# Gated attention feeding two expert layers on one core: scores issued behind the previous chunk's outputs, transposes of keys on their own, and PSUM shared out anew

## The chip, the cores and the metric

The kernel runs on one core of a Trainium2 chip. The metric is the device time of one execution in microseconds (us); before the change it is 919.28 us, the median of 3 runs (918.77 to 920.1). TensorE is called PE, VectorE DVE, ScalarE ACT, GpSimd POOL and SyncE SP.

## The reference

```python
f = 1 / (1 + exp(-f_logit))
for t in range(S):                                   # attention: B=4, H=8, S=768, D=48
    state = f[:, :, t, :, None] * state + k[:, :, t] (x) v[:, :, t]
    y[:, :, t] = q[:, :, t] @ state
x = y.transpose(0, 2, 1, 3).reshape(B * S, H * D)    # 3072 tokens, 384 wide
x = maximum(x @ w_in, 0)**2 @ w_out                  # layer 1, 384 -> 2048 -> 384
h = x @ w_in2                                        # layer 2, the same sizes
return where(h > 0, h, exp(minimum(h, 0)) - 1) @ w_out2
```

## The kernel before, in words

**Attention** is computed in 24 chunks g of 128 tokens, each with all 8 heads of one batch (batch g % 4), so the state that chunk g needs is that of chunk g-4. Heads lie in four pairs p, the two heads of a pair on partitions 0 to 47 and 64 to 111. For a chunk, `a_gate` and `a_decay` turn the logits into running products of decays, `a_scale` (L168) multiplies queries and keys by them, and `a_scores` first transposes the keys (L176, tile tp, four transposes) and then multiplies keys by queries (L182, tile sc, one matmul for each head). `a_transposed` (L187) copies tp to SBUF on ACT (kt), `a_mask` (L191) copies the causal half of the scores into ss on DVE. `a_carry` (L196) decays the state, `a_state` (L209) multiplies keys by values (tile kv), `a_add` (L218) adds that to the state on DVE. `a_out` sums two products into tile o: masked scores by values (L241) and state by queries (L248); ACT copies o to SBUF (L255), small DMAs on SP's queue put it in its place (L260), and `a_hi` and `a_lo` (L280, L288) split it into the two parts xh and xl that the layers read. Every fp32 matmul is issued as two instructions.

**The layers** run in 12 blocks of 512 tokens (6 of each layer) by 16 pieces f of 128 hidden features, 192 units in all. The main loop (L485 to L498) has one slot u for each unit: first the planned steps of slot u, then `up` of unit u (L360, nine matmuls of 128x128 by 512 columns into tile ph), `down` of unit u-2 (L412, nine matmuls into the three banks y), then `between` of unit u (L373 to L379 in layer 1: relu and square on ACT, gh on ACT in block 0) and `low` (gl; on DVE, L393, in block 0, on POOL, L399, later). In block 0 the weights of unit u+1 are also unpacked: `load_raw` (DMA), `decode_weights` (L52 on ACT, then L54, L57 and L58 on DVE, tile dec) and `split_weights`, whose high part is a copy on ACT (L329) and whose low part is a subtraction on DVE (L330) that reads the high part.

**The order** within an engine is the order of issue, written by hand: a table START for the first chunks and units, then `plan`, a list of steps for each slot. The table FIRST says at which slots of a block a chunk's steps begin (at 0, 3, 6 and 8 for chunks 4 to 7, all in block 0; for the chunks whose tokens block i takes, at -6, -2, 2 and 6 counted from the start of block i-1); the steps then follow slot by slot: gate, decay, scale and carry, (an empty slot,) scores with transposes and mask, state and outputs, add, nothing, hi and lo. Within a slot, the steps of chunks are issued ahead of those of the weights.

**PSUM**'s eight banks: two for ph of layer 1 (`ps_h`), three for y0, y1 and y2 (`ps_y`), and three in turn (`ps_a`) for everything else: tp, the two halves of sc, kv, the two halves of o, and ph of layer 2.

Of the kernel before, what the change touches and what calls it, by code (L numbers as in the profile page):

```python
# [11 lines left out]
F32 = mybir.dt.float32  # L12
# [24 lines left out]
FIRST = (0, 3, 6, 8), (-6, -2, 2, 6)  # L37
# [23 lines left out]
def chunked(ctx, tc, ff, qk, vk, vz, wraw, mask, ident, flag, out):  # L61
# [15 lines left out]
    ps_h = ctx.enter_context(tc.tile_pool(name="ps_h", bufs=2, space=PSUM))  # L77
    ps_y = ctx.enter_context(tc.tile_pool(name="ps_y", bufs=1, space=PSUM))
    ps_a = ctx.enter_context(tc.tile_pool(name="ps_a", bufs=3, space=PSUM))
# [89 lines left out]

    def a_scores(g):  # L170
        s = st[g]
        q, k = (s["qk"][:, o].rearrange("r (p t) -> r p t", p=NP) for o in range(2))
        if g < NG - B:
            s["tp"] = tp = ps_a.tile([128, NP, 128], F32, tag="a", name=f"tp{g}")
            for p in range(NP):
                PE.transpose(tp[:, p, 0:ROWS], k[:, p], idt[:ROWS, :ROWS])  # L176

        pool, tags = (ps_a, "aa") if g >= B else (ps_h, "hh") if g % 2 else (ps_y, ("y0", "y1"))
        s["sc"] = sc = [pool.tile([128, NP, 128], F32, tag=tags[j], name=f"sc{g}_{j}") for j in range(2)]
        for p in range(NP):  # L180
# [17 lines left out]
    def a_state(g):  # L198
        s = st[g]
        now = state[g % B]  # L200
        if g < NG - B:
            kvp = ps_a.tile([128, NP, 48], F32, tag="a", name=f"kv{g}")
            for p in range(NP):
                for j, (lo, hi) in enumerate(((0, 64), (64, ROWS))):
                    if g >= B:
                        v = s["vk"][:, p, j]
                    else:
                        v = s["vz"][:, p, at_(p, j), 0:48] if p < NK else s["vz"][:, :, at_(p, j), 96:112]
                    PE.matmul(kvp[lo:hi, p], s["kt"][:, p, lo:hi], v, start=True, stop=True)  # L209
            if g >= B:  # L210
                s["kv"] = kvp
            else:
                A.activation(now, kvp[:ROWS], AF.Copy)

    def a_add(g):
        if g < NG - B:
            now = state[g % B]
            V.tensor_tensor(out=now, in0=st[g]["kv"][:ROWS], in1=now, op=ALU.add)  # L218

    def a_direct(g):  # L220
        s = st[g]
        yp = ps_a.tile([128, NK, 128], F32, tag="a", name=f"yp{g}")
# [9 lines left out]
    def a_out(g):  # L232
# [20 lines left out]
        for i in (1, 0):  # L253
            for lo, hi in HD:
                A.activation(x1[lo:hi, 2 * i:2 * i + 2], o[i][lo:hi], AF.Copy)  # L255
# [405 lines left out]
```

## Time and profile before

| | before |
|---|---|
| runs | 920.1, 918.77, 919.28 us; median 919.28 |
| the profiled execution's own time | 917.91 us |
| its span | 916.1 us |
| PE busy | 890.3 us (97%) |
| DVE busy | 562.4 us (61%) |
| ACT busy | 440.8 us (48%) |
| POOL busy | 295.2 us (32%) |
| mean granted TensorE clock | 0.990 |

The profile is of one execution. Its span runs from the first to the last instruction; 1.8 us of the execution's own time lie around it. An engine's busy time counts the instructions that work on data; matmuls are pipelined, so the rows of PE overlap by the end of each. In a row of the timeline that stands for several instructions (x16), the first number is the start of the first, the second the time from there to the end of the last. Idle time stands at the end of a row in brackets, with what ended it.

### The profile page before, as it was taken

Reading aid. Unit: us, or ns where it says so; the run is one execution under the profiler, and the core shown is the slowest. Engines: PE = TensorE matmul, PEld = TensorE weight load, DVE = VectorE, ACT = ScalarE, POOL = GpSimd, SP = SyncE. Lnnn points to the kernel's source line nnn. Section 1 sums busy time; section 2 is a strip of 40 time slices with the busy share of each in tenths; the row PEclk is TensorE's granted clock in tenths of the full one; section 3 lists DMA queues with packets and bytes.
Section 4 is the critical chain, followed back from the end, with each engine's and each line's share of the span. In section 5 each row is a group of like instructions: output and inputs, shape, how many; then the busy total and the mean of one; then the engine's idle time right before and its main releaser. Section 6 shows DMA issues by size and latency. Waiting matters only on the chain.

```text
span 916.1 us, 13300 instructions
## 1 busy us (share of the span) xinstructions
PE 890.3 (97%) x5001; PEld 724.5 (79%) x5001; DVE 562.4 (61%) x837; ACT 440.8 (48%) x751; POOL 295.2 (32%) x243
## 2 busy tenths in 40 slices
PE   7799899999999999999999999999999999999997
PEld 5577688888888888788888888888888888888885
DVE  8899978677676676775300256555564565555543
ACT  4477655444544444444444444444544444444543
POOL 2111114444444344442333233332333323333231
PEclk8999999999999999999999999999999999999999
DMA  8556434334344533433256510100100100100001
GB/s 265 165 177 200 140 105 145 110 112 145 112 129 148 180 128 110 146 112 109 110 184 224 189 59 0 58 12 1 58 11 1 58 12 1 57 12 1 35 1 38
DMA packets 30791, 88.45 MB, mean 97 GB/s; under 512 B 4992, under 2 KB 9728, under 8 KB 30720
## 3 DMA queue, kind: packets, MB, share of 16 engines
q1 hardware_dynamic: 28848, 77.32, 25.5%
q10 hardware_dynamic: 1872, 10.22, 3.3%
q8 instruction: 40, 0.66, 0.3%
q14 instruction: 31, 0.25, 0.1%
HBM read 64.52 MB, written 22.02 MB: 94 GB/s over the span
## 4 chain that ended last, share of the span: by engine, by line
PE 92%; DVE 4%; DMA 1%; issue 1%; ACT 1%; SPq 0%; DVEq 0%
PE ph L360 42%; PE y L412 42%; PE sc L182 3%; PE o L241 2%; PE o L248 1%; DMA ff<-ff 1%; PE kv L209 1%; PE tp L176 1%; DVE ds L145 1%; DVE dec L57 1%; DVE w L330 0%; DVE qk L168 0%; PE yp L226 0%; DVE dec L58 0%; DVE gl L393 0%
## 5 line engine op out<-in xcount | busy, mean ns | idle before, releaser
L399 POOL TENSOR_TENSOR gl<-gg,gh 128x512 fp32r<-128x512 f32 x175 | 250.0, 1429 | 500.1 <-PE ph L360 192.2
L412 PE MATMUL y<-gh,wf 128*128 128x512 f32 (+1 forms) x582 | 177.9, 387 | 0.0
L412 PE MATMUL y<-gh,w 128*128 128x512 f32 x576 | 177.4, 389 | 0.0
L385 DVE SCALAR_TENSOR_TENSOR t<-r,t 128x512 f32<-128x512 f32 (+1 forms) x97 | 71.9, 742 | 158.8 <-ACT r L384 158.5
L360 PE MATMUL ph<-xh,w 128*128 128x512 f32 x576 | 155.5, 405 | 4.9 <-DVE w L330 3.1
L360 PE MATMUL ph<-xh,wf 128*128 128x512 f32 (+1 forms) x582 | 146.4, 387 | 0.0
L381 ACT ACTIVATE r<-ph 128x512 f32<-128x512 f32 (+1 forms) x97 | 57.6, 593 | 181.9 <-PE ph L360 177.0
L360 PEld LDWEIGHTS ph<-xh,w 128*128 128x128 f32 x576 | 106.0, 190 | 34.0 <-DVE w L330 4.6
L412 PEld LDWEIGHTS y<-gh,wf 128*128 128x128 f32 x582 | 108.9, 188 | 22.4 <-ACT gh L388 0.2
L360 PEld LDWEIGHTS ph<-xh,wf 128*128 128x128 f32 x582 | 108.6, 188 | 22.3
L412 PEld LDWEIGHTS y<-gh,w 128*128 128x128 f32 x576 | 108.1, 188 | 22.5
L412 PE MATMUL y<-gl,wf 128*128 128x512 f32 (+1 forms) x291 | 112.7, 387 | 0.0
L373 ACT ACTIVATE r<-ph 128x512 f32<-128x512 f32 x96 | 57.1, 595 | 114.6 <-PE ph L360 94.7
L412 PE MATMUL y<-gl,w 128*128 128x512 f32 x288 | 112.1, 389 | 0.0
L360 PE MATMUL ph<-xl,w 128*128 128x512 f32 x288 | 81.7, 392 | 1.9 <-DVE xl L286 1.9
L360 PE MATMUL ph<-xl,wf 128*128 128x512 f32 (+1 forms) x291 | 81.1, 387 | 0.0
L379 DVE TENSOR_TENSOR gh<-r 128x512 fp32r<-128x512 f32 x64 | 45.8, 716 | 49.4 <-ACT r L373 49.3
L386 DVE SCALAR_TENSOR_TENSOR gg<-ph,t 128x512 f32<-128x512 f32 (+1 forms) x97 | 66.6, 686 | 10.0
L360 PEld LDWEIGHTS ph<-xl,w 128*128 128x128 f32 x288 | 54.6, 190 | 14.2 <-DVE xl L286 2.4
L374 ACT ACTIVATE gg<-r 128x512 f32<-128x512 f32 x96 | 60.7, 633 | 7.7
L412 PEld LDWEIGHTS y<-gl,wf 128*128 128x128 f32 x291 | 54.6, 188 | 11.2 <-DVE gl L393 0.2
L360 PEld LDWEIGHTS ph<-xl,wf 128*128 128x128 f32 x291 | 54.4, 188 | 11.1
(73 smaller groups left out, 959.4 us busy)
## 6 DMA issues: line engine op xcount, KB each, us to landing
raw<-wraw SPq DMA_DIRECT2D x19, 768.0 KB, 4.7
wst<-w SPq DMA_DIRECT2D x16, 768.0 KB, 4.3
wf<-wst SPq DMA_DIRECT2D x16, 768.0 KB, 4.2
qk<-qk SPq DMA_DIRECT2D x24, 448.0 KB, 5.7
raw<-wraw ACTq DMA_DIRECT2D x13, 768.0 KB, 4.5
ff<-ff SPq DMA_DIRECT2D x22, 227.9 KB, 4.8
x2d<-yo SPq DMA_DIRECT2D x18, 256.0 KB, 2.3
x<-x2d SPq DMA_DIRECT2D x18, 256.0 KB, 3.2
```

The source lines that it names most:

```text
L57: V.scalar_tensor_tensor(out=out, in0=hi, scalar=0x80000000, in1=out, op0=ALU.bitwise_and, op1=ALU.bitwise_or)
L182: PE.matmul(sc[j][:, p], k[lo:hi, p], q[lo:hi, p], start=True, stop=True)
L241: PE.matmul(o[p // 2][r:r + 48, p % 2], s["vk"][:, p, j], ss[g % 2][:, j, p], start=p % 2 == 0, stop=False, skip_group_check=True,)
L360: PE.matmul(ph, w[:, a, 0, 128 * k:128 * k + 128], b[:, k, c], start=(m == 0), stop=(m == len(todo) - 1))
L373: A.activation(r[:, c], ph, AF.Relu)
L374: A.activation(gg[:, c], r[:, c], AF.Square)
L379: V.tensor_tensor(out=gh[:, c], in0=r[:, c], in1=r[:, c], op=ALU.mult)
L381: A.activation(r[:, c], ph, AF.Relu, scale=-1.0)
L385: V.scalar_tensor_tensor(out=t[:, c], in0=r[:, c], scalar=1.0, in1=t[:, c], op0=ALU.add, op1=ALU.mult)
L386: V.scalar_tensor_tensor(out=gg[:, c], in0=ph, scalar=0.0, in1=t[:, c], op0=ALU.max, op1=ALU.add)
L399: G.tensor_tensor(out=gl, in0=gg, in1=gh, op=ALU.subtract)
L412: PE.matmul(yp_[i][m][:, c], w[:, a, 1, 128 * m:128 * m + 128], b[:, c], start=(f == 0 and n_ == 0), stop=(f == NF - 1 and n_ == 2 and c.s ...
```

## The change

Steps move, and one kind of matmul is cut in two.

- **Scores** of chunk g+1 are issued inside `a_out` of chunk g, directly behind its outputs (argument `then`). Each head's matmul of 128 key columns becomes two of 64, so that the 16 products of a chunk (32 instructions) take the four 64x64 parts of the array in turn; before, 8 products (16 instructions) took two halves in turn.
- **Transposes** become a step of their own, `a_keys`, one slot ahead of the outputs; the copy to kt is issued with them. They go to the banks "o", or "s" where the next scores are four slots away.
- **The keys-by-values product** moves into `a_out` and into o's banks (columns 256 to 351); `a_add` reads it there.
- **The mask** is one instruction of 1024 columns a partition in place of two of 512.
- **PSUM**: three banks for y, two ("s") for the scores, two ("o") for the outputs, one ("h"); ph takes "h", "s" or "o" by `bank`.
- **The plan**: a table SCORES says at which slot a chunk's scores stand (3, 6, 9 and 11, as before, then 13, 17, 21 and so on, four apart); outputs stand at the slot of the next scores, so one or two slots later than before in block 0 and two later afterwards. From chunk 9 on gate, decay, scale, carry and scores stand one slot earlier than before, and everywhere hi and lo at most one later. The steps of a slot are sorted: add, keys, outputs, scores, then the weights' split, then scale, carry, mask, hi, lo, gate, decay; loads and unpacking come last. Before, the weights' split came behind the chunk's steps.
- The loads of logits and values come one slot earlier in the steady part, that of q and k stays in its slot; the flag at the end of the attention is raised one slot later. The table START is unchanged.

```diff
--- before
+++ after
-FIRST = (0, 3, 6, 8), (-6, -2, 2, 6)
+SCORES = (3, 6, 9, 11), (-3, 1, 5, 9)
...
-    ps_h = ctx.enter_context(tc.tile_pool(name="ps_h", bufs=2, space=PSUM))
-    ps_y = ctx.enter_context(tc.tile_pool(name="ps_y", bufs=1, space=PSUM))
-    ps_a = ctx.enter_context(tc.tile_pool(name="ps_a", bufs=3, space=PSUM))
+    ps_y = ctx.enter_context(tc.tile_pool(name="ps_y", bufs=3, space=PSUM))
+    ps = ctx.enter_context(tc.tile_pool(name="ps", bufs=1, space=PSUM))
...
+    def a_keys(g, tag):
+        if g < NG - B:
+            k = st[g]["qk"][:, 1].rearrange("r (p t) -> r p t", p=NP)
+            pool = ps_y if g < B else ps
+            tp = pool.tile([128, NP, 128], F32, tag=tag, name=f"tp{g}")
+            for p in range(NP):
+                PE.transpose(tp[:, p, 0:ROWS], k[:, p], idt[:ROWS, :ROWS])
+            st[g]["kt"] = kt = one.tile([128, NP, ROWS], F32, tag="kt", name=f"kt{g}")
+            if g < B:
+                st[g]["tp"] = tp
+            else:
+                A.activation(kt, tp[:, :, 0:ROWS], AF.Copy)
+    def a_transposed(g):
+        A.activation(st[g]["kt"], st[g]["tp"][:, :, 0:ROWS], AF.Copy)
     def a_scores(g):
         s = st[g]
+        if g < B:
+            a_keys(g, "y")
         q, k = (s["qk"][:, o].rearrange("r (p t) -> r p t", p=NP) for o in range(2))
-        if g < NG - B:
-            s["tp"] = tp = ps_a.tile([128, NP, 128], F32, tag="a", name=f"tp{g}")
-            for p in range(NP):
-                PE.transpose(tp[:, p, 0:ROWS], k[:, p], idt[:ROWS, :ROWS])
-        pool, tags = (ps_a, "aa") if g >= B else (ps_h, "hh") if g % 2 else (ps_y, ("y0", "y1"))
-        s["sc"] = sc = [pool.tile([128, NP, 128], F32, tag=tags[j], name=f"sc{g}_{j}") for j in range(2)]
+        s["sc"] = sc = ps.tile([128, 2, NP, 128], F32, tag="so"[g < B and g % 2], name=f"sc{g}")
         for p in range(NP):
-            for j, (lo, hi) in enumerate(HD):
-                PE.matmul(sc[j][:, p], k[lo:hi, p], q[lo:hi, p], start=True, stop=True)
-    def a_transposed(g):
-        if g < NG - B:
-            st[g]["kt"] = kt = one.tile([128, NP, ROWS], F32, tag="kt", name=f"kt{g}")
-            A.activation(kt, st[g]["tp"][:, :, 0:ROWS], AF.Copy)
+            for r in range(0, 128, 128 if g < B else 64):
+                e = slice(r, 128 if g < B else r + 64)
+                for j, (lo, hi) in enumerate(HD):
+                    PE.matmul(sc[e, j, p], k[lo:hi, p, e], q[lo:hi, p], start=True, stop=True)
...
     def a_mask(g):
-        for j, sc in enumerate(st[g]["sc"]):
-            V.copy_predicated(out=ss[g % 2][:, j], mask=msk.unsqueeze(1).to_broadcast([128, NP, 128]), data=sc)
+        V.copy_predicated(
+            out=ss[g % 2].rearrange("r j p t -> r (j p) t"), mask=msk.unsqueeze(1).to_broadcast([128, 2 * NP, 128]),
+            data=st[g]["sc"].rearrange("r j p t -> r (j p) t"),
+        )
...
     def a_add(g):
         if g < NG - B:
-            now = state[g % B]
-            V.tensor_tensor(out=now, in0=st[g]["kv"][:ROWS], in1=now, op=ALU.add)
+            now = state[g % B].rearrange("r (b i) d -> r b i d", b=2)
+            kv = st[g]["o"][:ROWS, :, 256:352].rearrange("r b (i d) -> r b i d", i=2)
+            V.tensor_tensor(out=now, in0=kv, in1=now, op=ALU.add)
...
-    def a_out(g):
+    def a_out(g, then):
         s = st[g]
         q = s["qk"][:, 0].rearrange("r (p t) -> r p t", p=NP)
-        o = [ps_a.tile([128, 2, 128], F32, tag="a", name=f"o{g}_{i}") for i in range(2)]
+        s["o"] = o = ps.tile([128, 2, 512], F32, tag="o", name=f"o{g}")
+        begun = set()
+        def mm(p, r, rows, c, n, *args):
+            key = p // 2, r
+            PE.matmul(
+                o[r:r + rows, p // 2, c:c + n], *args, start=key not in begun, stop=False, skip_group_check=True
+            )
+            begun.add(key)
+        if g < NG - B:
+            for p in (0, 2, 1, 3):
+                for j, (lo, hi) in enumerate(((0, 64), (64, ROWS))):
+                    mm(p, lo, hi - lo, 256 + 48 * (p % 2), 48, s["kt"][:, p, lo:hi], s["vk"][:, p, j])
         for p in (0, 2, 1, 3):
             for j in range(2):
-                r = 64 * at_(p, j)
-                PE.matmul(
-                    o[p // 2][r:r + 48, p % 2], s["vk"][:, p, j], ss[g % 2][:, j, p],
-                    start=p % 2 == 0, stop=False, skip_group_check=True,
-                )
+                mm(p, 64 * at_(p, j), 48, 128 * (p % 2), 128, s["vk"][:, p, j], ss[g % 2][:, j, p])
         for p in (0, 2, 1, 3):
             for j, (lo, hi) in enumerate(HD):
-                r = 64 * at_(p, j)
-                PE.matmul(
-                    o[p // 2][r:r + 48, p % 2], state[g % B][lo:hi, p], q[lo:hi, p],
-                    start=False, stop=p % 2 == 1, skip_group_check=True,
-                )
+                mm(p, 64 * at_(p, j), 48, 128 * (p % 2), 128, state[g % B][lo:hi, p], q[lo:hi, p])
+        if then:
+            a_scores(then)
...
+    slot = {g: 16 * (where[g][0] - 1) + SCORES[where[g][0] > 1][g % B] for g in range(B, NG)}
+    slot[NG] = slot[NG - 1] + 4
+    banks = {0: "h", 1: "s", 2: "o"}
+    for g in range(B, NG):
+        n = slot[g + 1] - slot[g]
+        for d, tag in enumerate({2: "hs", 3: "hsh", 4: "hsoh"}[n]):
+            banks[slot[g] + d] = tag
+    def bank(u, d):
+        return banks[u] if u in banks else "soh"[(u + d) % 3]
...
-        pool, tag = (ps_a, "a") if layer else (ps_h, "h")
         hs[i, f] = []
-        for c in pieces(i, f):
-            ph = pool.tile([128, c.stop - c.start], F32, tag=tag, name=f"ph{i}_{f}_{c.start}")
+        for d, c in enumerate(pieces(i, f)):
+            ph = ps.tile([128, c.stop - c.start], F32, tag=bank(NF * i + f, d), name=f"ph{i}_{f}_{c.start}")
...
-    prepare = (a_gate,), (a_decay,), (a_scale, a_carry)
-    finish = (a_scores, a_transposed, a_mask), (a_state, a_out), (a_add,), (), (a_hi, a_lo)
     for g in range(B, NG):
-        i, o = where[g]
-        d = o // 128
-        base = 16 * (i - 1) + FIRST[i > 1][d]
-        for d, f in enumerate(prepare + finish if i == 1 else (*prepare, (), *finish)):
-            for h in f:
-                at(base + d, h, g)
-        at(base - 1, load_f, g)
-        at(base - 1, load_qk, g)
-        at(base + 1, load_v, g)
+        i, s, then = where[g][0], slot[g], slot[g + 1]
+        early = g > 2 * B
+        at(s - 3 - early, a_gate, g)
+        at(s - 2 - early, a_decay, g)
+        at(s - 1 - early, a_scale, g)
+        at(s - 1 - early, a_carry, g)
+        if g == B:
+            at(s, a_scores, g)
+        at(s, a_mask, g)
+        at(then - 1, a_keys, g, "s" if then - s > 3 else "o")
+        at(then, a_out, g, g + 1 if g + 1 < NG else None)
+        at(then + 1, a_add, g)
+        at(then + 2, a_hi, g)
+        at(then + 2, a_lo, g)
+        at(s - 4 - early, load_f, g)
+        at(slot[g - 1] if g > B + 1 else s - 4, load_qk, g)
+        at(slot[g - 1] + 1 if g > B + 1 else s - 2, load_v, g)
     at(16 * (n1 - 1) + 1, least_decay)
-    at(16 * (n1 - 1) + 3, raise_flag)
+    at(16 * (n1 - 1) + 4, raise_flag)
     for f in range(NF):
         at(f - 3, load_raw, 0, f)
...
         for k in range(NK):
             at(16 * (i - 1) + 6 + 3 * k, load_x, i, k)
+    order = [a_add, a_keys, a_out, a_scores, split_weights, a_scale, a_carry, a_mask, a_hi, a_lo, a_gate, a_decay]
...
-            todo = plan.get(u, ())
+            todo = sorted(plan.get(u, ()), key=lambda t: order.index(t[0]) if t[0] in order else len(order))
```

**PE, a block of layer 1.** Here tp is the transposed keys, sc the scores, o the outputs, ph and y a unit's `up` and `down`. Before, the scores stand with the transposes between two units:

```order
L412 MATMUL y_2_477<-gl_15_1339,w_15_1237 128x512
L176 MATMUL tp_1426<-idt,qk_1179 128x112 x4
L182 MATMUL sc_0_1431<-qk_1179 128x128
L182 MATMUL sc_1_1432<-qk_1179 128x128
...
L182 MATMUL sc_0_1431<-qk_1179 128x128
L182 MATMUL sc_1_1432<-qk_1179 128x128
L360 MATMUL ph_2_0_1447<-xh_741,w_2_412 128x512 x6
L360 MATMUL ph_2_0_1447<-xl_742,w_2_412 128x512 x3
```

In the change the transposes stand alone, and the scores (L200) close the block of the outputs one unit later:

```order
L178 MATMUL tp_1527<-idt,qk_1206 128x112 x4
L390 MATMUL ph_4_0_1540<-xh_795,w_4_501 128x512 x6
L390 MATMUL ph_4_0_1540<-xl_796,w_4_501 128x512 x3
...
L252 MATMUL o_1567<-vk_1252,kt_1532 64x48
L252 MATMUL o_1567<-vk_1252,kt_1532 48x48
L252 MATMUL o_1567<-ss_90,vk_1252 48x128 x8
L252 MATMUL o_1567<-qk_1206,state_92 48x128 x8
L200 MATMUL sc_1592<-qk_1407 64x128 x16
L390 MATMUL ph_5_0_1630<-xh_795,w_5_541 128x512 x6
```

The eight products of 128 columns stood between the transposes and an `up`; sixteen of 64 columns (each again two instructions) now stand directly behind the matmuls of o.

**DVE, block 0, around slot 10.** gl is the last step of a unit, L330 (L349 in the change) the low part of the weights, dec the unpacking, qk the scaling, ss the mask. Before:

```order
L393 TENSOR_TENSOR gl_9_940<-gg_9_942,gh_9_939 128x512
L288 TENSOR_TENSOR xl_742<-x_5_772,xh_741 128x3x128
L168 TENSOR_TENSOR qk_795<-qk_795,ds_91 112x512 x2
L196 TENSOR_TENSOR state_97<-state_97,wc_901 112x192
L330 TENSOR_TENSOR w_11_992<-dec_11_913,w_11_992 128x768
L54 TENSOR_SCALAR dec_12_995<-dec_12_995 128x768
L57 SCALAR_TENSOR_TENSOR dec_12_995<-raw_12_918,dec_12_995 128x768
L58 SCALAR_TENSOR_TENSOR dec_12_995<-raw_12_918,dec_12_995 128x768
L393 TENSOR_TENSOR gl_10_1022<-gg_10_1024,gh_10_1021 128x512
L218 TENSOR_TENSOR state_96<-kv_949,state_96 112x192
L191 COPY_PREDICATED ss_93<-msk,sc_0_1035 128x512
```

and in the change:

```order
L423 TENSOR_TENSOR gl_9_931<-gg_9_933,gh_9_930 128x512
L227 TENSOR_TENSOR state_92<-o_835,state_92 112x192
L349 TENSOR_TENSOR w_11_946<-dec_11_904,w_11_946 128x768
L169 TENSOR_TENSOR qk_900<-qk_900,ds_88 112x512 x2
L211 TENSOR_TENSOR state_94<-state_94,wc_897 112x192
L55 TENSOR_SCALAR dec_12_956<-dec_12_956 128x768
L58 SCALAR_TENSOR_TENSOR dec_12_956<-raw_12_909,dec_12_956 128x768
L59 SCALAR_TENSOR_TENSOR dec_12_956<-raw_12_909,dec_12_956 128x768
L423 TENSOR_TENSOR gl_10_983<-gg_10_985,gh_10_982 128x512
L349 TENSOR_TENSOR w_12_1043<-dec_12_956,w_12_1043 128x768
L203 COPY_PREDICATED ss_90<-msk,sc_1015 128x1024
```

The weights' low part stood behind the chunk's scaling, carry and lo; it now stands directly behind gl and the add, ahead of them.

**ACT, block 0, slots 10 and 11.** kt is the copy of the transposed keys, x that of the outputs, w the high part of the weights, r, gg and gh a unit's `between`. Before:

```order
L280 ACTIVATE xh_741<-x_5_772 128x3x128
L255 ACTIVATE x_6_976<-o_1_959 48x256 x2
L255 ACTIVATE x_6_976<-o_0_958 48x256 x2
L134 ACTIVATE ff_906<-ff_906 112x521
L329 ACTIVATE w_11_992<-dec_11_913 128x768
L52 ACTIVATE dec_12_995<-raw_12_918 128x768
L316 DMA raw_13_1000<-wraw 128x768
L373 ACTIVATE r_10_1023<-ph_10_0_1002 128x512
```

and in the change:

```order
L183 ACTIVATE kt_944<-tp_939 128x448
L348 ACTIVATE w_11_946<-dec_11_904 128x768
L135 ACTIVATE ff_902<-ff_902 112x521
L53 ACTIVATE dec_12_956<-raw_12_909 128x768
L335 DMA raw_13_961<-wraw 128x768
L403 ACTIVATE r_10_984<-ph_10_0_963 128x512
L404 ACTIVATE gg_10_985<-r_10_984 128x512
L407 ACTIVATE gh_10_982<-r_10_984 128x512
L272 ACTIVATE x_6_1032<-o_990 48x256 x4
L348 ACTIVATE w_12_1043<-dec_12_956 128x768
```

In slot 10 the copy kt now stands ahead of the high part of w_11, and it reads a tile that PE writes after the add of slot 10; in slot 11 the copies x stand ahead of the high part of w_12, as they stood ahead of that of w_11 before.

## Rows read from the trace of the kernel before

**Rows 1.** Busy time by stage: PE, PEld, DVE, ACT, POOL (x count), clock, DMA, GB/s.

```profile
45.00:125.00 80.00, 72.05 (x544) 56.09 (x544) 78.33 (x119) 55.21 (x94) 9.36 (x13) 0.98 0.49 156
125.00:450.00 325.00, 325.00 (x2139) 263.21 (x2139) 222.48 (x315) 152.10 (x273) 132.61 (x104) 1.00 0.38 127
```

**Rows 2.** Timeline of PE, a chunk of the steady part: start us, us, work.

```profile
251.65 1.52 PE L360 MATMUL ph<-xh,w 128*128 128x512 f32 x6
...
255.73 1.52 PE L360 MATMUL ph<-xh,w 128*128 128x512 f32 x6
...
259.82 0.55 PE L176 MATMUL tp<-idt,qk 112*128 112x112 f32 x4
260.30 1.16 PE L182 MATMUL sc<-qk 48*128 48x128 f32 x16
261.39 1.65 PE L360 MATMUL ph<-xh,w 128*128 128x512 f32 x6
...
266.09 0.30 PE L241 MATMUL o<-ss,vk 128*48 128x128 f32 x1
...
266.19 1.04 PE L241 MATMUL o<-ss,vk 128*48 128x128 f32 x15
267.16 0.65 PE L248 MATMUL o<-qk,state 48*48 48x128 f32 x16
267.75 1.66 PE L360 MATMUL ph<-xh,w 128*128 128x512 f32 x6
```

**Rows 3.** Transposes of that chunk by line L176: least, median and most ns.

```profile
L176 PE MATMUL tp<-idt,qk x4: 258/259/261, 259.8 to 260.1; 112*128 112x112 f32 x4
```

**Rows 4.** Timeline of PE at the end of block 0.

```profile
105.64 0.61 PE L209 MATMUL kv<-vk,kt 128*64 128x48 f32 x15
...
113.58 1.45 PE L360 MATMUL ph<-xh,w 128*128 128x512 f32 x5 [1.02 <-DVE w L330]
...
125.55 1.66 PE L360 MATMUL ph<-xh,w 128*128 128x512 f32 x6
```

**Rows 5.** Timeline of DVE in block 0.

```profile
38.31 0.68 DVE L393 TENSOR_TENSOR gl<-gg,gh 128x512 fp32r<-128x512 f32 x1
39.30 0.96 DVE L330 TENSOR_TENSOR w<-dec,w 128x768 fp32r<-128x768 f32 x1 [0.31 <-ACT w L329]
...
46.19 1.28 DVE L168 TENSOR_TENSOR qk<-qk,ds 112x512 f32<-112x512 f32 x2
47.39 0.35 DVE L196 TENSOR_TENSOR state<-state,wc 112x192 f32<-112x192 f32 x1
47.66 0.95 DVE L330 TENSOR_TENSOR w<-dec,w 128x768 fp32r<-128x768 f32 x1
...
54.12 0.55 DVE L54 TENSOR_SCALAR dec<-dec 128x768 uint32<-128x768 uint32 x1
...
57.22 0.07 DVE L144 MEMSET lim<- 112x9 f32 x1
...
122.84 0.94 DVE L330 TENSOR_TENSOR w<-dec,w 128x768 fp32r<-128x768 f32 x1
123.70 0.67 DVE L393 TENSOR_TENSOR gl<-gg,gh 128x512 fp32r<-128x512 f32 x1
```

**Rows 6.** Timeline of ACT in block 0.

```profile
38.43 0.84 ACT L329 ACTIVATE w<-dec 128x768 fp32r<-128x768 f32 x1 [0.95 <-DVE dec L58]
...
49.52 0.52 ACT L187 ACTIVATE kt<-tp 128x448 f32<-128x448 f32 x1
...
107.83 1.57 ACT L255 ACTIVATE x<-o 48x256 f32<-48x256 f32 x4 [2.28 <-PE o L248]
```

**Rows 7.** PE's sequencer by line L176, and then by line L209, 61 to 69 us.

```profile
L176 PEldq EVENT_SEMAPHORE  x1: 4335/4335/4335, 61.3 to 61.3; - x1
...
L209 PEldq EVENT_SEMAPHORE  x1: 51/51/51, 67.3 to 67.3; - x1
```

More of the change, by code (lines that the diff above doesn't have):

```diff
@@ L199, in a_state @@
         s = st[g]
-        now = state[g % B]
[L201 to L213, printed above, removed]
+        kvp = ps_y.tile([128, NP, 48], F32, tag="y", name=f"kv{g}")
+        for p in range(NP):
+            for j, (lo, hi) in enumerate(((0, 64), (64, ROWS))):
+                v = s["vz"][:, p, at_(p, j), 0:48] if p < NK else s["vz"][:, :, at_(p, j), 96:112]
+                PE.matmul(kvp[lo:hi, p], s["kt"][:, p, lo:hi], v, start=True, stop=True)
+        A.activation(state[g % B], kvp[:ROWS], AF.Copy)
     def a_add(g):
         if g < NG - B:
-            now = state[g % B]
-            V.tensor_tensor(out=now, in0=st[g]["kv"][:ROWS], in1=now, op=ALU.add)
+            now = state[g % B].rearrange("r (b i) d -> r b i d", b=2)
+            kv = st[g]["o"][:ROWS, :, 256:352].rearrange("r b (i d) -> r b i d", i=2)
+            V.tensor_tensor(out=now, in0=kv, in1=now, op=ALU.add)
     def a_direct(g):
         s = st[g]
-        yp = ps_a.tile([128, NK, 128], F32, tag="a", name=f"yp{g}")
+        yp = ps_y.tile([128, NK, 128], F32, tag="y", name=f"yp{g}")
         for k in range(NK):
@@ L230, in a_direct @@
         s["yp"] = yp
-    def a_out(g):
+    def a_out(g, then):
         s = st[g]
         q = s["qk"][:, 0].rearrange("r (p t) -> r p t", p=NP)
-        o = [ps_a.tile([128, 2, 128], F32, tag="a", name=f"o{g}_{i}") for i in range(2)]
+        s["o"] = o = ps.tile([128, 2, 512], F32, tag="o", name=f"o{g}")
[8 more added lines that the diff above has]
+            for p in (0, 2, 1, 3):
+                for j, (lo, hi) in enumerate(((0, 64), (64, ROWS))):
+                    mm(p, lo, hi - lo, 256 + 48 * (p % 2), 48, s["kt"][:, p, lo:hi], s["vk"][:, p, j])
         for p in (0, 2, 1, 3):
             for j in range(2):
-                r = 64 * at_(p, j)
-                PE.matmul(
-                    o[p // 2][r:r + 48, p % 2], s["vk"][:, p, j], ss[g % 2][:, j, p],
-                    start=p % 2 == 0, stop=False, skip_group_check=True,
-                )
+                mm(p, 64 * at_(p, j), 48, 128 * (p % 2), 128, s["vk"][:, p, j], ss[g % 2][:, j, p])
         for p in (0, 2, 1, 3):
             for j, (lo, hi) in enumerate(HD):
-                r = 64 * at_(p, j)
-                PE.matmul(
-                    o[p // 2][r:r + 48, p % 2], state[g % B][lo:hi, p], q[lo:hi, p],
-                    start=False, stop=p % 2 == 1, skip_group_check=True,
-                )
+                mm(p, 64 * at_(p, j), 48, 128 * (p % 2), 128, state[g % B][lo:hi, p], q[lo:hi, p])
+        if then:
+            a_scores(then)
         x1 = two.tile([128, NK + 1, 128], F32, tag="x1", name=f"x1_{g}")
@@ L254, in a_out @@
             for lo, hi in HD:
-                A.activation(x1[lo:hi, 2 * i:2 * i + 2], o[i][lo:hi], AF.Copy)
+                A.activation(
+                    x1[lo:hi, 2 * i:2 * i + 2], o[lo:hi, i, 0:256].rearrange("r (p t) -> r p t", p=2), AF.Copy
+                )
             if i:
@@ L303, in raise_flag @@
     def raise_flag():
-        tp = ps_a.tile([1, ROWS], F32, tag="a", name="mt")
+        tp = ps.tile([1, ROWS], F32, tag="o", name="mt")
         PE.transpose(tp, mrow, idt[:ROWS, :ROWS])
@@ L407, in down @@
         if f == 0:
-            yp_[i] = [ps_y.tile([128, n], F32, tag=f"y{m}", name=f"y{i}_{m}") for m in range(NK)]
+            yp_[i] = [ps_y.tile([128, n], F32, tag="y", name=f"y{i}_{m}") for m in range(NK)]
         for c in pieces(i, f):
@@ L468, in chunked @@
         G.memset(ss[1], 0.0)
-        warm = ps_a.tile([128, 512], F32, tag="a", name="warm")
+        warm = ps_y.tile([128, 512], F32, tag="y", name="warm")
         for _ in range(3):
```

## The prediction, made before the changed kernel had run

> **What bounds the kernel now.** I read the busy time by stage first: it says which engine to follow where. From 125 us on PE is busy for 325.00 of 325 us [rows 1], and the timeline shows unit after unit without idle time before them: there only fewer or shorter steps of PE count. From 45 to 125 us, while block 0 unpacks its weights, DVE is busy for 78.33 of 80 us and PE for 72.05 [rows 1]. A plain unit costs DVE 0.86 us for the weights' low part (122.84 to 123.70) and 3.10 for unpacking and gl (54.12 to 57.22) [rows 5], together 3.96, about what a unit takes on PE; attention's steps come on top. So DVE sets the pace, and PE waits for it, as in the 1.02 us before 113.58 that the low part of w ended [rows 4]. Block 0 has to be read on DVE and on ACT, which feeds it; the rest on PE. All sums stand against the profiled execution, 917.91 us, which is 1.37 below the median of the runs, 919.28; I add that at the end. A measurement here can tell about 0.2%, 1.84 us, from no change.
>
> **The steady part, on PE.** A plain unit takes 255.73 - 251.65 = 4.08 us. Transposes and scores stand from 259.82 to 261.39, 1.57 us, and the six matmuls behind them take 1.65 instead of 1.52, so a chunk pays 1.70 for both [rows 2]. In the change four transposes stand alone: they start (260.1 - 259.8)/3, about 0.10 us, apart [rows 3], and from the timeline's 0.55 less one duration of 0.26 the step is 0.097, so 4 x 0.097 = 0.39. Bounds: nothing lost on leaving them for a unit gives 0.39; the whole 0.48 to the next start (260.30) and the 0.13 that the scores lost on leaving give 0.61. I take the low end, since they start and end with matmuls that use nearly all rows, as a unit's do. The thirty-two score instructions go four at a time: eight steps, as the eight pairs were. A step is (1.16 - 0.30)/7.5 = 0.115 for the old pairs, (1.04 - 0.30)/7 = 0.106 for the pairs of o and (0.65 - 0.30)/3 = 0.117 for the state's products, which run four at a time on parts of the array, the form the new ones have; 0.30 is one such matmul's duration [rows 2]. I take 0.11: 0.88 us, bounds 0.85 and 0.94. They follow the state's products without leaving that form, and the end of the block is paid once, as before. So four parts in place of two buys no steps; the gain is the change of form that falls away: 1.70 - 0.39 - 0.88 = 0.43 a chunk, between 0.15 and 0.46. For chunks 9 to 23 that is 15 x 0.43 = 6.45 us (2.3 to 6.9).
>
> Against that stands work that crosses from block 0, where PE has time, to the steady part: the transposes and outputs of chunk 8 stood ahead of unit 15's `up` and now stand behind it, 0.39 + (267.75 - 261.39 - 4.08 = 2.28) = 2.67 us [rows 2]. Net after unit 15: **-3.78 us**.
>
> The rest of the steady part I cost at nothing. The mask (one instruction, 1.3 us as two were) frees its banks within the unit that follows the scores, the add and the copies of x within two; these have 4.08 and 8.16 us, and DVE works 222.48, ACT 152.10 of 325 us [rows 1]. If that cover failed, PE would stand before the next `up`, by what the mask is late. The copy kt (0.52 [rows 6]) has a unit. On SP's queue the loads of q and k stand behind six placements of x, which wait for its copies, some 3 us; scaling stands two units and a chunk's outputs later. POOL's steps move a slot and nobody waits for them (132.61 of 325 busy).
>
> **Block 0, on DVE.** Before unit 15's `up`, DVE has the same work in both kernels. What changes is that the low part of the weights (which needs ACT's high part, which needs the unpacked weights) now stands first in its slot, and no longer behind scaling, carry or mask. The cover goes:
> - Slot 2: today scaling and carry fill 46.19 to 47.66 [rows 5]. Without them DVE waits for the high part, which starts some 0.1 us behind the unpacking and takes 0.84 [rows 6]: 0.95 us.
> - Six slots whose low part now stands directly behind gl: the row at 39.30 shows such a place today, with 0.31 idle [rows 5]; with the gap after a wait, 0.35 each: 2.1 us. Two slots with an add between gl and the low part keep 0.1 each: 0.2.
> - Slots 10 and 12. Here the add frees bank "o", only then PE transposes (0.55, [rows 2]), ACT copies kt (0.52), then comes to the high part (0.84 [rows 6]), and DVE waits all of that, 1.91 and 0.1 to start: 2.0 each, 4.0 us.
> - Slots 11 and 13. ACT's copies of x stand ahead of the high part. They start 2.19 us behind the first matmul of the outputs' block (105.64 [rows 4] to 107.83 [rows 6]) and take 1.5. Counted from the end of the add one slot earlier: transposes 0.47, `up` and `down` 4.08, a gap 0.1, 2.19, 1.5, high part 0.84 = 9.2. DVE's own work from there is 2.0 + 0.86 + 1.20 + 0.27 + 3.10 = 7.4 [rows 5]. It waits 1.85 each: 3.7 us.
>
> Sum D = 0.95 + 2.1 + 0.2 + 4.0 + 3.7 = 10.95 us of new idle time on DVE. The low part of w15 is done at 123.70 and unit 15 starts at 125.55 [rows 4, 5], so 1.85 us are covered: unit 15 starts 9.1 us later. D's bounds: nothing, if every high part is ready; 12 to 13, if the later waits are a little longer. Total: 9.1 - 3.78 = **+5.3 us**, 923.2 for this execution, **924.6** against the median.
>
> One rule of the Trainium skill speaks against the block of scores. The sequencer's row first: between two events, 65.64 (61.3 + 4.335) and 67.3, it passed the 38 matmuls of transposes, scores and a unit, at most 44 ns each with their weight loads [rows 7]. At that rate the new block's 80 matmuls take 3.5 us; the array needs 2.28 + 0.88 less some 0.4 at the ends, 2.8, and the sequencer has run ahead during the unit before, so I charge nothing. The page "TensorE: Matmul & The Clock Gate", section "Wait — 56ns, not 53.3ns?", says that a sequencer that decodes in software spends about 62 ns on a matmul. By that the block takes 5.0 us less what is queued, and some 2 us a chunk would be lost, an estimate; the row's 44 ns speaks against that rate.
>
> **The rivals.**
> - *The two chains don't bite.* If at slots 10 to 13 the bank is free, or PE is so far behind DVE that transposes and copies come anyway while DVE is busy, each of the four waits is the usual 0.35. D = 0.95 + 2.1 + 0.2 + 1.4 = 4.65; 4.65 - 1.85 - 3.78 = -0.98: **918.3**. For it: PE itself waits for DVE, so its place moves with DVE. Against it: the add, and what it releases, stand one behind the other on three engines, with nothing else for DVE in between.
> - *Faster.* One mechanism: ACT's high part is there whenever DVE asks for the low one, because gl or a wait before it takes longer than ACT's 0.84. Then D is 0, unit 15 starts 1.85 earlier as chunk 8's outputs no longer stand before it, and the total is -1.85 - 3.78 = -5.63: **913.6**. It decides below D = 5.63, and shows as faster below 3.8. For it: ACT is busy for only 55.21 of 80 us [rows 1]. Against it: in the row at 39.30 the wait is there today, and DVE's idle time of today, 1.67 us in that stretch, is less than one chunk's new waits.
> - *Four at a time isn't had.* The scores go in sixteen steps (8 x 0.11 more a chunk), or the sequencer has nothing queued (3.5 - 2.8 = 0.7 more). Over 15 chunks that is 13 or 11 us: **936 to 938**. The state's products speak against both: 16 instructions on four parts in 0.59 us, 37 ns each [rows 2].
>
> **How the numbers follow.** Forecast 0.57; chains that don't bite 0.16; faster 0.22; no four at a time 0.05. The forecast's own range: with D = 8 and a gain of 6.9 the total is +1.9, with D = 11 and a gain of 2.3 it is +9.5, so 921.2 to 928.8. The range reaches down to 914.5, which leaves out the extreme of the faster case and, above, what passes 928.8: together about 0.15. Slower by over 0.2% are the forecast and the last rival, 0.62; within 0.2% the first rival, 0.16; faster 0.22.
>
> **What would show it.** Right: DVE's low parts in block 0 with idle time ended by ACT's high part, 2 us in slots 10 and 12; unit 15's `up` some 9 us later; afterwards PE without idle time and 0.4 us less a chunk, the block of outputs and scores at about 3.2 us beyond a unit. Wrong: unit 15 no later than 127 us; transposes that cost clearly more than 0.4 alone; PE idle before the `up` that follows the scores.

## The result, and the profile after

The change makes the kernel slower: 927.8 us median (926.73 to 929.07, 4 runs) against 919.02 of the kernel before measured beside it, a ratio of 1.0097 (95% interval 1.0084 to 1.011). The forecast was slower, 924.6 in a range from 914.5 to 928.8.

The profiled execution took 928.62 us, span 926.8: 10.7 more than the span of before. PE was busy for 888.8 us, DVE for 577.7. The busy time by stage, in the columns of [rows 1], shows where it went:

```profile
45.00:125.00 80.00, 60.57 (x466) 47.90 (x465) 67.59 (x97) 44.23 (x74) 9.07 (x12) 0.88 0.46 142
140.00:450.00 310.00, 310.00 (x2365) 254.09 (x2366) 232.21 (x295) 151.09 (x270) 114.36 (x101) 1.00 0.40 132
```

From 45 to 125 us, within block 0, DVE now stands idle for 12.4 of 80 us (1.7 before) and PE for 19.4 (8.0 before); from 140 to 450 us PE is never idle, as before. So the loss is made in block 0. The groups of DVE from 40 us to unit 15's `up` (busy us, mean ns | idle us before them and what ended it) name one wait. The row by itself below is the same group in the kernel before, up to its unit 15:

```profile
L349 DVE TENSOR_TENSOR w<-dec,w 128x768 fp32r<-128x768 f32 x14 | 13.4, 959 | 15.0 <-ACT w L348 14.9
...
L423 DVE TENSOR_TENSOR gl<-gg,gh 128x512 fp32r<-128x512 f32 x14 | 9.6, 684 | 0.0
...
L203 DVE COPY_PREDICATED ss<-msk,sc 128x1024 f32<-128x1024 int32 x5 | 6.6, 1321 | 0.0
```

```profile
L330 DVE TENSOR_TENSOR w<-dec,w 128x768 fp32r<-128x768 f32 x14 | 13.3, 948 | 0.3 <-ACT w L329 0.3
```

The new idle time is the low part of the weights waiting for ACT's high part. The timeline of DVE has the single waits; they answer to the rows of L330 in [rows 5]:

```profile
48.44 0.96 DVE L349 TENSOR_TENSOR w<-dec,w 128x768 fp32r<-128x768 f32 x1 [0.91 <-ACT w L348]
...
54.24 0.96 DVE L349 TENSOR_TENSOR w<-dec,w 128x768 fp32r<-128x768 f32 x1 [0.31 <-ACT w L348]
...
100.47 0.35 DVE L227 TENSOR_TENSOR state<-o,state 112x192 f32<-112x192 f32 x1
103.29 0.96 DVE L349 TENSOR_TENSOR w<-dec,w 128x768 fp32r<-128x768 f32 x1 [2.47 <-ACT w L348]
...
112.40 0.96 DVE L349 TENSOR_TENSOR w<-dec,w 128x768 fp32r<-128x768 f32 x1 [3.20 <-ACT w L348]
...
123.78 0.96 DVE L349 TENSOR_TENSOR w<-dec,w 128x768 fp32r<-128x768 f32 x1 [2.47 <-ACT w L348]
...
132.92 0.96 DVE L349 TENSOR_TENSOR w<-dec,w 128x768 fp32r<-128x768 f32 x1 [3.65 <-ACT w L348]
...
138.93 0.96 DVE L349 TENSOR_TENSOR w<-dec,w 128x768 fp32r<-128x768 f32 x1
```

Four waits, in slots 10 to 13, make 11.8 us. What stands behind the first pair is seen on PE and on ACT:

```profile
94.93 0.39 PE L442 MATMUL y<-gl,w 128*128 128x512 f32 x1
100.97 0.98 PE L178 MATMUL tp<-idt,qk 112*128 112x112 f32 x4 [5.65 <-DVE state L227]
101.62 2.91 PE L390 MATMUL ph<-xh,w 128*128 128x512 f32 x6
104.33 1.41 PE L390 MATMUL ph<-xl,w 128*128 128x512 f32 x3
```

```profile
101.98 0.55 ACT L183 ACTIVATE kt<-tp 128x448 f32<-128x448 f32 x1 [6.84 <-PE tp L178]
...
102.42 0.83 ACT L348 ACTIVATE w<-dec 128x768 fp32r<-128x768 f32 x1
...
109.92 1.19 ACT L272 ACTIVATE x<-o 48x256 f32<-48x256 f32 x3 [2.29 <-PE o L252]
...
111.52 0.85 ACT L348 ACTIVATE w<-dec 128x768 fp32r<-128x768 f32 x1
```

PE's next instruction is the transposes, and they wait 5.65 us for the add (100.47 on DVE), which frees their bank; behind them stand the unit, kt and the high part. In the slot behind, the copies of x, which follow that late unit, keep ACT from the next high part.

A chunk of the steady part, for [rows 2]:

```profile
263.50 0.55 PE L178 MATMUL tp<-idt,qk 112*128 112x112 f32 x4
263.81 1.64 PE L390 MATMUL ph<-xh,w 128*128 128x512 f32 x6
...
269.59 0.65 PE L252 MATMUL o<-qk,state 48*48 48x128 f32 x16
270.06 1.05 PE L200 MATMUL sc<-qk 48*64 48x128 f32 x32
271.05 1.66 PE L390 MATMUL ph<-xh,w 128*128 128x512 f32 x6
...
283.42 0.55 PE L178 MATMUL tp<-idt,qk 112*128 112x112 f32 x4
```

Four units with a chunk take 283.42 - 263.50 = 19.92 us. In the timeline of before, the transposes behind those of [rows 2] are

```profile
280.13 0.55 PE L176 MATMUL tp<-idt,qk 112*128 112x112 f32 x4
```

and 280.13 - 259.82 = 20.31: the change saves 0.39 us a chunk. Chunks 20 to 23 have no transposes; there a chunk with its four units took 19.46 us (scores at 361.46 and 380.92) and now takes 19.01 (387.23 and 406.24, its outputs), 0.45 less. Unit 15's `up` starts at 139.53, 13.98 later than in [rows 4], and the end is 10.7 later, so 3.3 us were won back.

### The profile page after: what moved, and what is told of

Read it like the earlier page. It is cut to its first block, busy times and chain, and to the rows that moved or that the text cites. A ratio compares the mean times of both kernels' runs of the same rounds, so it can differ in the third digit from the quotient of the medians.

```text
span 926.8 us, 13934 instructions
## 1 busy us (share of the span) xinstructions
PE 888.8 (96%) x5321; PEld 728.3 (79%) x5321; DVE 577.7 (62%) x813; ACT 442.4 (48%) x751; POOL 281.5 (30%) x243
## 4 chain that ended last, share of the span: by engine, by line
PE 88%; DVE 6%; DMA 2%; ACT 2%; issue 1%; SPq 1%; ACTq 0%; DVEq 0%
PE ph L390 40%; PE y L442 40%; PE o L252 4%; PE sc L200 2%; DVE dec L58 1%; DVE dec L59 1%; DMA ff<-ff 1%; PE tp L178 1%; DVE w L349 1%; SPq L279 1%; DMA qk<-qk 1%; ACT w L348 1%; DVE dec L55 1%; DVE ds L146 1%; PE yp L235 0%
## 5 line engine op out<-in xcount | busy, mean ns | idle before, releaser
L429 POOL TENSOR_TENSOR gl<-gg,gh 128x512 fp32r<-128x512 f32 x175 | 236.3, 1351 | 453.5 <-PE ph L390 190.8
L390 PE MATMUL ph<-xh,w 128*128 128x512 f32 x576 | 157.4, 409 | 3.9 <-ACT w L348 2.5
L390 PEld LDWEIGHTS ph<-xh,w 128*128 128x128 f32 x576 | 108.5, 194 | 31.0 <-issue 3.8
L442 PEld LDWEIGHTS y<-gl,w 128*128 128x128 f32 x288 | 54.1, 188 | 11.3
```

What stands on the lines that cost most here:

```text
L390: PE.matmul(ph, w[:, a, 0, 128 * k:128 * k + 128], b[:, k, c], start=(m == 0), stop=(m == len(todo) - 1))
L429: G.tensor_tensor(out=gl, in0=gg, in1=gh, op=ALU.subtract)
L442: PE.matmul(yp_[i][m][:, c], w[:, a, 1, 128 * m:128 * m + 128], b[:, c], start=(f == 0 and n_ == 0), stop=(f == NF - 1 and n_ == 2 and c.s ...
```

## The experiments

The theory was the prediction's: new idle time on DVE in block 0, most of it made at slots 10 to 13 by transposes that wait for the add, less a gain of 0.4 us a chunk afterwards. The rivals: the order of the weights' split alone; or something outside block 0 (banks, start, feeding). The ten runs stand here by what they test. The `up` of unit 16 starts at 129.77 us in the kernel before and 14.5 us later in the change.

### The split last again

```diff
-    order = [a_add, a_keys, a_out, a_scores, split_weights, a_scale, ..., a_decay]
+    order = [a_add, a_keys, a_out, a_scores, a_scale, ..., a_decay, split_weights]
```

> The changed kernel with one line different: in the order of a slot's steps the weights' split stands last again, behind scaling, carry, mask, hi, lo and decay. My theory (the loss is DVE waiting in block 0 for the weights' high part): the waits of 0.9 us in slot 2 and of 0.31 in six slots go, 2.8 us; at slots 10 to 13 only about 1.1 us of each pair goes, because gl and the mask then wait for the same chain through PE (add, transposes, units). Together some 5 us: 923, between 921 and 925. Rival 1, the order of the split is all of it: 917 or less. Rival 2, the loss lies elsewhere (start, banks, feeding of the array): 927 to 929.

927.17 us (ratio to before 1.0092, 1.0074 to 1.0109): not 923. The groups of DVE up to its unit 15:

```profile
L349 DVE TENSOR_TENSOR w<-dec,w 128x768 fp32r<-128x768 f32 x13 | 12.4, 953 | 3.5 <-ACT w L348 3.5
L423 DVE TENSOR_TENSOR gl<-gg,gh 128x512 fp32r<-128x512 f32 x13 | 9.3, 717 | 1.2 <-ACT gh L407 1.2
...
L203 DVE COPY_PREDICATED ss<-msk,sc 128x1024 f32<-128x1024 int32 x5 | 6.6, 1326 | 5.4 <-PE sc L200 5.4
```

The waits fell from 15.0 to 10.1 us, the 5 us that were expected, and the rest moved to gl and the mask. Unit 16 came only 2.7 us earlier, though, because with the split last the decay of chunk 9 stands ahead of w15's low part, 2.9 us on DVE that I had not counted: unit 15 stood 2.12 us for that low part (the same is shown further down). By the medians the gain is 0.6 us; the two profiled executions lie 0.8 above and 1.3 below theirs. By its time alone the run fits rival 2; what speaks against that rival is the trace and two runs further down, the old plan in block 0 and the bank. The order alone is not the loss: the transposes still waited for the add, 6.3 and 4.9 us.

### Transposes behind the unit; the same with the high part first and the low part last

```diff
+            keys = [t for t in todo if t[0] is a_keys and u < 16]
...
                 between(*units[u])
+                for f, args in keys:
+                    f(*args)
                 low(*units[u])
```

> The changed kernel with one thing different: in block 0 the transposes of keys and their copy are issued at the end of their slot, behind the unit's matmuls, instead of ahead of them; the split still stands first. My theory: PE no longer stands still before a unit for the add, ACT's high part is no longer behind kt or late copies of x, and PE's clock stays at its upper level; the waits of 2.5 and 3.2 to 3.7 us at slots 10 to 13 (11.8 us in all) fall to 0.3 each or less, the small ones of slots 2 to 9 stay. Unit 15 starts some 3 us later than in the kernel before, in place of 14, and the steady part gives that back: 919, between 917 and 921. Rival, the waits come from the order of the split alone: 925 or more.

929.23 us (1.0108, 1.0091 to 1.0124). In the next run, moreover, `split_weights` was cut into a step for ACT, first in the slot, and one for DVE, last.

> The changed kernel with the split cut into its two steps: the high part (ACT) is issued first in the slot, the low part (DVE) last, and the transposes of keys in block 0 behind the unit's matmuls as in the run before. My theory: nearly no new idle time on DVE is left, unit 15 starts between 2 us earlier and 1 us later than in the kernel before, and the gain of the steady part (about 3.1 us net of chunk 8's crossing) is left: 915, between 913.5 and 917. Rival, the steady part has no real gain or the start of the program is slower by itself: 919 or more.

926.21 us (1.0072, 1.0054 to 1.009). Both miss the theory, by 10 and 11 us. By their times they fit the rivals, but not by the causes these give: against the order alone speaks the run before, against a steady part without gain the old plan in block 0 further down. In the second the wait for the high part is gone and another stands in its place:

```profile
L354 DVE TENSOR_TENSOR w<-dec,w 128x768 fp32r<-128x768 f32 x13 | 12.6, 970 | 0.3 <-ACT w L349 0.3
...
L203 DVE COPY_PREDICATED ss<-msk,sc 128x1024 f32<-128x1024 int32 x5 | 6.6, 1320 | 8.1 <-PE sc L200 8.1
```

and on PE, the outputs in front of those scores wait for kt:

```profile
105.48 0.98 PE L252 MATMUL o<-vk,kt 128*64 128x48 f32 x15 [3.15 <-ACT kt L183]
```

With the transposes at the end of the slot, kt stands behind the unit's relu and squares on ACT. Here too unit 15 stood 2.17 us for w15's low part, which stood last, behind the decay of chunk 9. In the first run PE waited for kt four times, 2.2 to 3.3 us, the copies of x came later by as much, and DVE's waits for the high part stayed at 15.9 us. In these runs whatever lies between transposes and mask is one chain: moving a step backwards in it moved the wait.

### The order of the change in the plan of before

```diff
-            todo = plan.get(u, ())
+            front = (a_add, a_scores, a_transposed, a_state, a_out, split_weights)
+            todo = sorted(plan.get(u, ()), key=...)
```

> The kernel before with only the order of steps within a slot taken from the change: add, scores, outputs, then the weights' split, and scaling, carry, mask, hi, lo, gate and decay behind it; matmuls, banks and slots as before. My theory: DVE waits 0.9 us in slot 2, 0.31 in some five slots, and in the slots after a mask (4, 7, and less in 10 and 12) for a high part that stands behind copies of x, which now follow a later mask: 3 us twice and 0.5 twice. Some 10 us in all, less 1.85 covered: 927, between 922 and 929. Rival, the order alone is harmless and the new places of keys and outputs make the loss: 918 to 920.

942.11 us (1.0247, 1.0226 to 1.0267): the sign was right, the size not (+23 instead of +8). DVE's groups show the wait I named, over twice as long:

```profile
L330 DVE TENSOR_TENSOR w<-dec,w 128x768 fp32r<-128x768 f32 x13 | 12.6, 967 | 21.2 <-ACT w L329 21.2
```

In the old plan the split ahead of the mask is much worse than the change itself. The single waits show where the rest of the 21 us lies. In the slots behind a mask they are 4.45, 4.03, 3.45 and 2.72 us, where 3, 3, 0.5 and 0.5 were expected; in the slots of the scores, where kt stands ahead of the high part, 1.54, 1.55, 1.56 and 1.04 for 0.31. Before the transposes of its four chunks PE stood idle for 7.35, 6.02, 6.65 and 3.88 us, and the granted clock behind the first two was 0.50 (51 to 58 us) and 0.57 (78 to 84 us). So the transposes came late here as well, but for another reason: the trace puts the first and the last of these waits down to the chunk's scaling on DVE, which now stands behind the split.

### The plan of before in block 0 alone

```diff
+    for g in range(B, 2 * B):
+        base = (0, 3, 6, 8)[g % B]
+        finish = (a_keys, a_scores, a_mask), (a_out,), (a_add,), (), (a_hi, a_lo)
...
-    for g in range(B, NG):
+    for g in range(2 * B, NG):
...
+            if u >= NF:
                 todo = sorted(todo, key=...)
```

Transposes go to bank "h" there.

> The changed kernel with the plan of before in block 0 alone: chunks 4 to 7 have their transposes beside their scores, outputs in the slot behind, and the order of steps of before, with the weights' split last; scores of chunk 8 stand alone in slot 13; from unit 16 on everything is as in the change, banks and start too. Theory A (the loss is made in block 0, by the chain from add over transposes, copy, outputs and scores to the mask or the high part; the steady part gains 0.4 a chunk): unit 15 starts within 2 us of where it starts in the kernel before, and the steady part brings 3.3 us net: 915.5, between 913.5 and 918. Rival B (banks, start or feeding cost something anywhere): 919 or more.

918.71 us, 0.9995 of before (0.9986 to 1.0005): the loss is gone, though banks, start and feeding are the change's; but the gain was not there either. Unit 15 had to stop for the low part of w15:

```profile
124.62 0.39 PE L390 MATMUL ph<-xh,w 128*128 128x512 f32 x1
127.51 1.43 PE L390 MATMUL ph<-xh,w 128*128 128x512 f32 x5 [2.50 <-DVE w L349]
```

On DVE the decay of chunk 9, 123.60 to 126.51, stood ahead of it; in the plan of before it stands a slot later. The follow-up puts the split ahead of it in that slot:

```diff
-            if u >= NF:
+            if u >= NF or u == NF - 2:
```

> The run with the old plan in block 0 once more, with one step moved: in slot 14 the weights' split is issued ahead of chunk 9's decay (2.9 us on DVE), which in the kernel before stood a slot later. In the earlier run that decay stood ahead of the low part of w15, and unit 15's matmuls waited for it until 127.5. Theory A: the low part of w15 is done 2.9 us earlier, unit 15 runs through from about 124.6, and the 3.3 us of the steady part are left: 916, between 914.5 and 917.5, clearly faster than before. Rival: something else holds unit 16 up (chunk 7's low part, which now stands behind the decay), and it stays at 918 to 919.

914.57 us, 0.9949 (0.9936 to 0.9961): faster than both kernels. Unit 15 runs through from 123.59, 1.96 us ahead of [rows 4], and up to PE's last matmul (903.97 us for 909.12) the rest of the program adds 3.2. The banks of the steady part, the start and the feeding are the change's, so rival B is out.

```profile
123.59 1.76 PE L390 MATMUL ph<-xh,w 128*128 128x512 f32 x6
```

### The split first of all, transposes between up and down

The transposes' loop of the second run stands between `up` and `down`, and `split_weights` stands first in `order` (in every block, not in block 0 alone as the expectation says).

> The changed kernel with two things different in block 0: the weights' split is issued ahead of everything in its slot, so that ACT's high part no longer stands behind kt or the copies of x and DVE's low part is ahead of the add; and the transposes and kt are issued between a unit's up and down, ahead of the unit's relu on ACT, so that a late add holds up neither up nor the copy. Theory A (it is the length of the chain): DVE's waits for the high part stay at 0.3 in most slots and 0.9 in slot 2, those of 2.5 to 3.7 go, and the mask waits less than 1 us: 918.5, between 916.5 and 921. Rival (whatever is moved in front lets another wait take its place, as in the runs before): 925 or more.

923.62 us (1.0047, 1.0032 to 1.0063), between theory and rival, so it decides for neither: the long waits for the high part are gone (4.9 us in all are left), but the outputs of slot 9 waited 4.12 us for kt and the transposes of slot 12 still 3.46 for the add.

### Two at a time, and four at a time in the kernel before

```diff
-            for r in range(0, 128, 128 if g < B else 64):
-                e = slice(r, 128 if g < B else r + 64)
+            for r in range(0, 128, 128):
+                e = slice(r, 128)
```

> The changed kernel with scores as 8 products of 128 columns, two at a time, in place of 16 of 64 columns, four at a time; all else as in the change. My theory: eight steps either way, so the only difference is a change of the array's form between the state's products and the scores, 0.1 to 0.2 us a chunk: 928 to 931. Rival, four at a time halves the scores: 0.5 us more a chunk, 935 or more. Rival, half as many instructions are fed faster: 926 or less.

931.89 us (1.0135, 1.012 to 1.0151), 4.1 above the change. PE in the steady part:

```profile
250.44 0.65 PE L252 MATMUL o<-qk,state 48*48 48x128 f32 x16
251.02 1.16 PE L200 MATMUL sc<-qk 48*128 48x128 f32 x16
252.11 1.67 PE L390 MATMUL ph<-xh,w 128*128 128x512 f32 x6
```

The state's products take 0.58 to the next start instead of 0.47, the scores 1.09 instead of 0.99: 0.21 a chunk. From transposes to transposes a chunk takes 20.16 us (264.53 to 284.69) for 19.92, 3.6 us over 15. I read the 0.11 as the change of form between the two; the 0.10 lies in the scores themselves; together slightly above what I had allowed. The Trainium skill ("TensorEngine Tiling (Array Packing)", "Key Properties") says that a change of tiling mode, other than one of tile, drains the engine; the 0.11 us agrees with that, though no run here separates a drain from other costs of the step. The opposite edit, sixteen products of 64 columns in the kernel before:

> The kernel before with one thing from the change: scores as 16 products of 64 columns, four at a time, where they stood, behind the transposes. My theory: eight steps as before, the same changes of form on both sides: no difference, 918 to 920. Rival, four at a time is worth something by itself: 916.5 or less, with the block of scores clearly under 1.09 us. Rival, the sequencer can't feed thirty-two short ones: 924 or more.

918.37 us, 0.9995 (0.9986 to 1.0004), with

```profile
259.52 1.10 PE L184 MATMUL sc<-qk 48*64 48x128 f32 x32
260.55 1.66 PE L362 MATMUL ph<-xh,w 128*128 128x512 f32 x6
```

1.03 us for the scores. So four at a time is worth almost nothing by itself, 0.06 us a chunk here; behind the state's products, which already have that form, it was worth 0.21.

### Only the transposes' bank

```diff
-        at(then - 1, a_keys, g, "s" if then - s > 3 else "o")
+        at(then - 1, a_keys, g, {2: "h", 3: "o", 4: "s"}[then - s])
```

> The changed kernel with one thing different: where the next scores are two slots away (slots 10 and 12) the transposes of keys go to bank h, which the unit before has left, and no longer to o, which the add of that slot frees. Order, slots and all else as in the change. Theory A (the prediction's step: transposes wait for the add, and unit, kt, high part and copies of x wait behind them): DVE's waits at slots 10 and 12 fall from 2.5 to under 0.3 each, those at slots 11 and 13 from 3.2 and 3.7 to 0.3, PE keeps its upper clock, about 10 us in all: 918, between 916 and 920.5. Rival (the chain from add to outputs is only pushed one slot on, as in the runs that moved the transposes): 923 or more.

916.65 us, 0.9969 (0.9957 to 0.998): 11 us faster than the change, and faster than the kernel before. Slot 10 on PE, and the two low parts that waited 2.47 and 3.20 us in the change:

```profile
92.81 0.39 PE L442 MATMUL y<-gl,w 128*128 128x512 f32 x1
93.04 0.55 PE L178 MATMUL tp<-idt,qk 112*128 112x112 f32 x4
93.36 1.64 PE L390 MATMUL ph<-xh,w 128*128 128x512 f32 x6
```

```profile
98.76 0.96 DVE L349 TENSOR_TENSOR w<-dec,w 128x768 fp32r<-128x768 f32 x1
...
104.99 0.96 DVE L349 TENSOR_TENSOR w<-dec,w 128x768 fp32r<-128x768 f32 x1 [0.31 <-ACT w L348]
```

The transposes follow the unit before at once, the unit does not stand still, and kt and the copies of x are done before ACT's high part can start. DVE's waits up to unit 15 fall from 15.0 to 4.0 us. Order, slots and feeding are those of the change, so these 11 us are the bank's. The rival was not all wrong: PE's wait for the add did move one slot on, to the outputs, which waited 1.11 us in slot 11 and 2.39 in slot 13 (starts at 98.82 and 113.99). Each start lies 0.10 behind the end of the add, which frees their bank; the trace names ACT's high part, which ended at the same moment and which they do not read. The wait is shorter there, and DVE's in the same slots are 0.31 and 0.80 us. In slots 12 and 13 PE's clock did not hold all the time: 0.91 from 108 to 126 us.

## Why the prediction was right, and which term was too small

- **Where.** Right: the loss in block 0, on DVE's low parts, ended by ACT; PE without idle time afterwards; no loss where scores follow outputs. That the transposes' bank is the cause is shown by the run that changes nothing else.
- **D**, the new idle time, was put at 10.95 us and measured 14.7 (15.0, less the 0.3 that was there before). Slot 2: 0.91 for 0.95. Six low parts behind gl: 0.31 each for 0.35. Slots 10 and 12: 2.47 each for 2.0. Slots 11 and 13: **3.20 and 3.65 for 1.85 each**, and this is the mis-sized term. (The sum for it, 9.2 less 7.4, gives 1.8; the 0.05 changes nothing.) From the end of the add (100.82) to the low part (112.40) the chain took 11.6 us, for 9.2; DVE's own work and its earlier wait took 8.4 of them, for 7.4. I took PE's durations from rows at its upper clock. But PE had stood idle for 5.65 and 6.42 us before the transposes, and it came back at the lower one. By stretch, PE's busy time (second number) and granted clock (third number from the end):

```profile
95.00:101.00 6.00, 0.35 (x3) 0.07 (x2) 5.68 (x9) 0.14 (x1) 1.35 (x2) 0.81 0.56 155
101.00:105.00 4.00, 4.00 (x12) 3.32 (x13) 1.71 (x2) 2.63 (x4) 0.86 (x1) 0.50 0.45 140
105.00:112.00 7.00, 7.00 (x97) 5.62 (x97) 4.13 (x7) 3.76 (x8) 0.00 (x0) 0.96 0.17 47
```

  0.50 is the level of 1.2 GHz. The transposes took 0.65 to the next start where 0.31 is usual, the unit's `up` 3.96 (101.62 to 105.58) where 2.2 is: 2.1 us more in each chain. The transposes, 0.98 us instead of 0.55 to their end, make the wait in slots 10 and 12 longer by 0.4; the rest reaches slots 11 and 13. No run holds the clock alone fixed, so the 2.1 us are read from the rows.
- **Luck.** 14.7 lies above the prediction's own bound for D, 12 to 13. The time still fell into the range, 1.0 us below its upper end, because that end pairs D = 11 with a gain of only 2.3 us, and nearly the whole gain came.
- **The cover**, 1.85 us: about right. In the change the low part of w15 starts 16.09 us later (138.93 for 122.84) and unit 15 13.98 later, so 2.1 us were covered. The run with the old plan and the decay behind, with hardly a new wait, reached unit 15 1.96 us earlier; its unit 0 was 0.23 earlier already.
- **The start.** In the profiled execution unit 0 began at 31.41 us, 0.93 later than before, of which I had nothing. The last run has the same start and began it at 30.09; the other traces with the change's start lie between 30.25 and 31.94 us, the two others with the start of before at 30.33 and 30.64. So part of this belongs to the execution, whose time lies 0.8 above the median of the change; whether the start itself lost something is not shown. 0.93 + 14.7 - 1.85 is 13.8 of the 13.98; with the 2.1 that were covered it is 13.5, and 0.5 stays open.
- **The steady part.** -3.78 forecast, -3.3 measured. The sum charged chunks 20 to 23 for transposes that they do not have, which made little difference, as they gain 0.45. Transposes alone: 0.31 and 0.12 in the unit behind, 0.43 for 0.39. Scores: 0.99 less the 0.12 that the state's products no longer lose, 0.87 for 0.88. A gain of 0.39 for 0.43 a chunk.
- **The rivals.** The chains did bite; the high part was not ready. Four at a time was had: 32 instructions in 0.99 us, 31 ns each, and no gap in the block of 80. By the figure of the Trainium skill that I weighed ("TensorE: Matmul & The Clock Gate", "Wait — 56ns, not 53.3ns?": some 62 ns on a matmul decoded in software) the scores alone would have taken 2.0 us, an estimate; the trace does not bear out that rate here, and no run shows which way this engine decodes.

My remedies were less well judged than the forecast: I read the waits as what the order costs, and four re-orderings moved the time between 1.4 us more and 4.2 us less; the change of the bank alone gave back 11.

## What to carry to other kernels

When steps are moved, ask of each first instruction on an in-order engine which buffer it needs and who frees it: in this kernel a tile that was freed by a lagging engine stopped everything behind it, on three engines. Give such a tile a buffer that is long free before moving steps, and if the chain lets PE stand idle, work it out again with the durations that PE's rows show at the lower clock. And when a wait is taken away, look for the next one in the same chain before counting its length as a gain.

## What the runs showed of the hardware

After some 6 us with PE almost idle (0.35 us busy from 95 to 101 us), its next 4 us ran at a granted clock of 0.50, and the same matmuls of 512 columns took about 1.8 times as long; in the run with the other bank the stretch of the same two slots (91 to 108 us) has a clock of 1.00. Score products of 48x64, which take quarters of the array, started 0.47 us after the first of the state's products, which take quarters too; score products of 48x128, which take halves, started after 0.58 us.
